# Sums of the first output chunks in the main stage, and the last batch's combine weights in the slot stage

## The chip, the cores and the metric

The kernel runs on one NeuronCore of a Trainium2 chip. TensorE (PE) multiplies, VectorE (DVE), ScalarE (ACT) and GpSimd (POOL) do the rest, and SyncE (SP) issues the transfers. The metric is the device time of one launch in microseconds, with all inputs in HBM at the start and the output there at the end. Everything is float32.

## The reference, cut to what matters

Agent attention over four batches of 11456 tokens (49 agents, 128 channels) is followed by a soft mixture of experts (32 slots, 8 experts) over all 45824 rows:

```python
def sm(a, b):
    s = scale * (a @ b.transpose(0, 2, 1))
    e = np.exp(s - s.max(-1, keepdims=True))
    return e / (e.sum(-1, keepdims=True) + 1e-09)
x = (sm(q, agents) @ (sm(agents, k) @ v)).reshape(B * S, D)
logits = x @ phi                                    # 45824 x 32
d = np.exp(logits - logits.max(0)); d /= d.sum(0) + 1e-09   # over the rows
slot_out[e] = np.maximum((d.T @ x)[e] @ w1[e], 0) @ w2[e]   # 8 experts, 4 slots each
c = np.exp(logits - logits.max(1)); c /= c.sum(1) + 1e-09   # over the slots
return c @ slot_out
```

The *combine weights* are c: for each row the maximum over 32 slots, the exponential, the sum and the division.

## The kernel before, in words

Rows are handled in *cells* of 128; a batch has 90 cells, so there are 360. The logits of all of them stay in SBUF as `x_all` (128 partitions, 360 cells, 32 slots), and become the combine weights in place.

The program has three stages.

- **Main stage.** For each of four batches, k and v come in groups of up to 20 cells (steps whose names begin with k) and q in 24 groups of up to 16 cells (names that begin with q, group number behind the @). `qs` multiplies q with the agents, `qt` transposes on DVE, `qm` takes the row maximum; in odd groups `qu` subtracts it on POOL, `qe` is the exponential on ACT and `qw` the sum on DVE; `qr` and `qR` are the reciprocal, `qg` the division on POOL, `qp`, `qc` and `ql` lead to the logits, `qM` and `qn` take their maximum and transpose them into `x_all`. `r1` to `r4` join the maxima of a round of one or two groups, `ru` subtracts on POOL, `re` is the exponential and `rg` multiplies into the slot sums. Of the k steps, `km` and `kM` are maxima, `kr` and `kR` the running maximum (`kR` writes `nm`), `ku` adds it, `kE` multiplies with v and `kA` accumulates.
- **Slot stage.** `nm`, `wt`, `gl`, `gm`, `l0` to `l4`, `f0` to `f2` and `d0` to `d2` join the slot sums of all batches; `l4` writes `si`, the slots' inputs. Then come the experts: `mh` (product with w1), `mr` (ReLU), `mt` and `mc` (transpose and copy), `mo` (product with w2), `sb` and `sd`; `sd` is an ACT instruction that writes `sob`, the scaled slot outputs, for which the first output product waits. `fl` are products that fill PE's waits.
- **Output.** 25 chunks of up to 16 cells (`CHUNKS` is 4, 12, then 21 times 16, 4, 4): four products with `sob` (tile `po`), copies out of PSUM on DVE (a quarter) and ACT (three quarters) into `ot`, and a transfer of up to 1 MB.

Around the combine weights there are these steps. `cr@i` takes the row maxima of group i (DVE, tile `rm`, or `rms` for the last batch, groups 18 to 23), `cu@i` subtracts them (POOL), and `ce@i` is the exponential (ACT). For the first seven output chunks (`NORM = 7`, 96 cells, all of the first batch and six cells of the second) `os@j` sums and inverts on DVE (`o_sum`: a TENSOR_REDUCE, a TENSOR_SCALAR that adds 1e-9, a RECIPROCAL; tile `cd`), `om@j` multiplies on POOL (`o_mul`), and for the first four `ot@j` transposes on DVE (`o_tr`, tile `ct`; the output buffer has the tile name `ot`). The later chunks do these three inside the output loop.

Every engine runs its own instructions in order. That order is written out by hand in the string `ORDER`, one token for each step; a step stands there after all that it depends on, and each engine gets its steps in that order. Buffers are given out along the same order.

Of the kernel before, what the change touches and what calls it, by code (L numbers as in the profile page):

```python
# [53 lines left out]
kM@3 kt kA qp.0@0 kr qx@3 qr@2 kt qR@2 qc.0@0 kR qg.0@2 kr qc.1@0 kb kR kn qg.1@2 ka@4 kb ku.0
qp.0@2 ka@3 kn ku.1 ke.0 kx@5 qp.1@2 qc.0@2 ku.0 kE.0@3 qc.1@2 ku.1 ke.1 qs.0@3 ke.1 ke.0
qs.1@3 kv@5 qt.0@3 kE.1 qt.1@3 qm@3 ks.0@5 kA qu@3 cx ks.1@5 km.0@5 qx@4 qe@3 kE.0@4 km.1@5
qw@3 kE.1 kM@5 qr@3 qR@3 kt kx@6 qg.0@3 kA kr kg.1 qg.1@3 kg.2 qp.0@3 kh.1 kh.2 kg.3 qs.0@4
kh.4 kh.3 kb kv@6 ql@0 qt.0@4 kn ql@1 ku.0 qc.0@3 qn.0@0 qs.1@4 ke.0 qM.0@1 qn.1@0 qM.0@0
kE.0@5 ku.1 qx@5 qM.1@0 ke.1 ks.0@6 qt.1@4 qm@4 kx@7 kE.1 km.0@6 qE.0 qM.1@1 ql@2 r1@0 kA r2@0
qn.0@1 ks.1@6 qM.1@2 qM.0@2 qn.1@2 kv@7 r3@0 qE.1 qp.1@3 qn.0@2 ru.0@0 km.1@6 qs.0@5 kM@6  # L60
qn.1@1 kt qt.0@5 ru.1 ks.0@7 kr kR cr@1 re.0@0 qr@4 qR@4 qx@6 re.1 cu@1 kb qs.1@5 km.0@7 kn
qc.1@3 rg.0@0 ku.0 qg.0@4 ka@6 rg.1 ce@1 ku.1 ql@3 ke.0 qg.1@4 qt.1@5 qp.0@4 ke.1 kx@8 qn.0@3
ks.1@7 qM.1@3 rc@0 qc.0@4 qm@5 qM.0@3 qu@5 r1@1 kE.0@6 km.1@7 qe@5 kM@7 cr@2 r2@1 kE.1 kv@8
r3@1 qn.1@3 ru.0@1 cr@3 qs.0@6 kA cr@0 cu@2 re.0@1 qs.1@6 qt.0@6 cu@0 qw@5 rg.0@1 ce@2 qx@7 kt
qt.1@6 ks.1@8 ru.1 ce@0 kr kR qr@5 qR@5 ka@7 qm@6 kb ks.0@8 cu@3 re.1 r4@1 kx@9 r4@0 kn qE.0
# [54 lines left out]
fl r4@11 qn.1@21 rg.0@10 qn.0@21 fl cr@21 ru.1 re.0@11 fl fl fl nm os@1 wt fl rg.0@11 cu@21  # L120
re.1 l0 fl f0 os@6 rc@11 f1 fl rg.1 om@1 ce@21 os@4 fl rc@10 fl gl om@6 ot@1 gm l1 d0 fl om@4
# [947 lines left out]
```

## Time and profile before

| | |
|---|---|
| Median of 3 runs | 320.97 us (319.19 to 323.69) |
| Profiled execution, its own time | 321.17 us |
| Its span, first to last instruction | 318.9 us |
| Mean granted TensorE clock | 0.931 |
| Busy share of the span | PE 84%, DVE 78%, ACT 59%, POOL 42% |
| Moved by the transfers | 104.20 MB, 23.59 MB of it the output |

Times in the rows below are microseconds from the span's start. A row of the timeline has start, duration, engine, line, operation, output<-input with shapes, count, and in brackets how long the engine had been idle before it and who released it. A row of the table by stretches has for each engine the busy time and the instructions in brackets, then PE's granted clock, the transfers' share of 16 DMA engines, and GB/s. Line numbers are those of the kernel before.

### The profile page before, as it was taken

The page shows a single profiled execution, that of the slowest core. Times are in us where ns is not written, and L with a number is a line of the kernel's source. Part 1 is how long each engine was busy: PE and PEld are TensorE (multiplying, and loading weights), DVE is VectorE, ACT ScalarE, POOL GpSimd, SP SyncE. Part 2 cuts the span into 40 slices and gives each one's busy share as a digit, 9 for nine tenths or more (in the row PEclk, how much of TensorE's full clock was granted, in tenths as well). Part 3 has the DMA queues.
Part 4 walks back from the last instruction along what each step waited for, and adds up shares of the span by engine and source line. Part 5 has one row for each costly group of instructions (what it writes and reads, how often), then busy time and mean ns, then how long its engine had stood idle before and what let it go on. Part 6 is the DMA issues. An engine that isn't in the chain of part 4 may idle for free.

```text
span 318.9 us, 11055 instructions
## 1 busy us (share of the span) xinstructions
PE 266.3 (84%) x4522; PEld 169.4 (53%) x4522; DVE 248.1 (78%) x598; ACT 189.4 (59%) x623; POOL 132.5 (42%) x166
## 2 busy tenths in 40 slices
PE   3799999997698998988999998998898876766850
PEld 3638668665554776664666775565574632111210
DVE  1357767897769986988999988988999659989830
ACT  1125791492754985558589568698663255655550
POOL 1012223064505552566444490476897404434300
PEclk9999999999989999999999999999999997767555
DMA  7999999999979999867996899746930049999997
GB/s 250 400 402 390 398 396 402 401 397 400 394 250 376 399 393 368 301 260 295 377 377 264 252 360 384 244 175 237 419 141 3 2 164 422 415 415 420 420 419 286
DMA packets 31298, 104.20 MB, mean 327 GB/s; under 512 B 3601, under 2 KB 7825, under 8 KB 27537
## 3 DMA queue, kind: packets, MB, share of 16 engines
q1 hardware_dynamic: 31248, 103.52, 84.4%
q8 instruction: 35, 0.57, 0.7%
q14 instruction: 15, 0.11, 0.1%
HBM read 79.91 MB, written 23.59 MB: 325 GB/s over the span
## 4 chain that ended last, share of the span: by engine, by line
PE 45%; DVE 26%; DMA 10%; ACT 9%; issue 5%; POOL 2%; SPq 0%; DVEq 0%; POOLq 0%; ACTq 0%
PE sk L252 10%; PE ev L351 8%; PE sq L466 8%; DMA out<-ot 7%; PE tp L522 5%; ACT pt L494 4%; PE po L1002 3%; DVE pt L472 3%; PE lq L535 3%; DVE kmx L305 2%; ACT ot L1007 2%; DVE cd L852 2%; DVE ot L1006 2%; DMA w1s<-w 2%; DVE mx L477 2%
## 5 line engine op out<-in xcount | busy, mean ns | idle before, releaser
L494 ACT ACTIVATE pt<-pt,mx 128x49 f32<-128x49 f32 x192 | 61.6, 329 | 10.2 <-DVE mx L477 10.2
L513 POOL TENSOR_TENSOR pt<-pt,rt 128x392 f32<-128x392 f32 (+1 forms) x48 | 38.7, 809 | 46.1 <-DVE rt L508 25.2
L252 PE MATMUL sk<-ag,kt 128*64 128x49 f32 x1440 | 51.7, 230 | 6.6 <-DMA kt<-kT 4.3
L252 PEld LDWEIGHTS sk<-ag,kt 128*64 128x64 f32 x1440 | 48.8, 145 | 11.6 <-DVE ag L183 4.1
L466 PE MATMUL sq<-qt,ag 128*32 128x512 f32 (+1 forms) x384 | 49.6, 607 | 1.8 <-DVE et L339 1.1
L1002 PE MATMUL po<-ct,sob 32*128 32x512 f32 (+2 forms) x200 | 37.8, 838 | 15.6 <-DVE ct L865 11.3
L351 PE MATMUL ev<-vt,et 128*64 128x129 f32 x720 | 46.8, 277 | 1.7 <-issue 1.4
L1007 ACT COPY ot<-po 128x1536 f32<-128x1536 f32 (+2 forms) x25 | 32.8, 1311 | 23.3 <-DVE ot L1006 23.2
L351 PEld LDWEIGHTS ev<-vt,et 128*64 128x64 f32 x720 | 40.3, 138 | 9.6 <-issue 5.6
L472 DVE STREAM_TRANSPOSE pt<-sq 128x512 f32<-128x512 f32 (+1 forms) x48 | 31.9, 669 | 12.5 <-PE sq L466 12.0
L635 POOL TENSOR_TENSOR dt<-x_all,mbs 128x512 f32<-128x512 f32 (+1 forms) x24 | 29.2, 1227 | 28.8 <-DVE mbs L626 24.9
L859 POOL TENSOR_TENSOR x_all<-x_all,cd 128x512 f32<-128x512 f32 (+2 forms) x25 | 24.0, 961 | 38.0 <-DVE cd L854 37.3
L482 POOL TENSOR_TENSOR pt<-pt,mx 128x784 f32<-128x784 f32 (+1 forms) x12 | 16.2, 1353 | 55.4 <-DVE mx L477 53.1
L494 ACT ACTIVATION_READ_ACCUMULATOR pt<-pt,mx 128x1 f32 x192 | 37.0, 193 | 0.0
L529 ACT COPY pT<-tp 128x512 f32<-128x512 f32 (+1 forms) x48 | 25.7, 557 | 13.1 <-PE tp L522 11.0
L1002 PEld LDWEIGHTS po<-ct,sob 32*128 32x128 f32 x200 | 10.8, 247 | 42.5 <-ACT ot L1007 42.1
L522 PE MATMUL tp<-cs,pt 128*128 128x128 f32 x180 | 27.9, 286 | 5.9 <-issue 4.2
L305 DVE TENSOR_REDUCE kmx<-sk 128x49 f32<-128x490 f32 x32 | 20.7, 658 | 13.8 <-PE sk L252 13.6
L344 ACT ACTIVATE et<-et 128x490 f32<-128x490 f32 x36 | 21.6, 619 | 11.2 <-DVE et L339 11.1
L522 PEld LDWEIGHTS tp<-cs,pt 128*128 128x128 f32 x180 | 19.5, 142 | 15.1 <-issue 9.0
L339 DVE TENSOR_TENSOR et<-sk,kmb 128x490 f32<-128x490 f32 x36 | 22.5, 653 | 2.9 <-ACT kmb L329 2.8
L1006 DVE COPY ot<-po 128x512 f32<-128x512 f32 (+2 forms) x25 | 15.7, 629 | 11.4 <-DMA out<-ot 7.5
(111 smaller groups left out, 396.6 us busy)
## 6 DMA issues: line engine op xcount, KB each, us to landing
out<-ot SPq DMA_DIRECT2D x21, 1024.0 KB, 7.4
qt<-qT SPq DMA_DIRECT2D x44, 448.0 KB, 7.4
vt<-vL SPq DMA_DIRECT2D x36, 451.5 KB, 7.4
kt<-kT SPq DMA_DIRECT2D x35, 448.0 KB, 6.7
kt<-kT SPq DMA_DIRECT2D x17, 384.0 KB, 6.9
vt<-vL SPq DMA_DIRECT2D x16, 387.0 KB, 8.1
w2s<-w SPq DMA_DIRECT2D x4, 1024.0 KB, 6.9
w1s<-w SPq DMA_DIRECT2D x4, 1024.0 KB, 10.5
```

The source lines that it names most:

```text
L252: t_.matmul(sp[r:r + 64, c - c0, :], xt[:, P * c + r:P * c + r + 64], ag[:, b, 0:A], start=True, stop=True)
L305: v_.tensor_reduce(out=o_, in_=sp.rearrange("p c a -> p a c"), axis=AX.X, op=ALU.max)
L351: t_.matmul(k["ev"][o_:o_ + 64, :], k["e"][:, c, :], k["v"][:, c, :], start=c < 2, stop=c >= n - 2)
L466: t_.matmul(q["s", h][32 * r_:32 * r_ + 32, :nt], ag[:, b, 32 * h:32 * h + 32], q["x"][:, r_, :], start=True, stop=True)
L472: v_.transpose(out=q["pt"][:, :n, 32 * h:32 * h + 32], in_=q["s", h][:, :nt].rearrange("p (t a) -> p t a", a=32))
L494: s_.activation(out=x, in_=x, func=AF.Exp, bias=q["mx"][:, c:c + 1], accum_out=q["dn"][:, c:c + 1])
L513: nc.gpsimd.tensor_tensor(out=x, in0=x, op=ALU.mult, in1=q["rt"][:, c0:c1].unsqueeze(2).to_broadcast([P, c1 - c0, A]))
L522: t_.transpose(q["tp", h][:, (c - c0) // 2, :], q["pt"][:, c:c + 2, :].rearrange("p c a -> p (c a)"), ident)
L529: s_.copy(out=q["pT"][:, c0 // 2:c1 // 2, :], in_=q["tp", h][:, :(c1 - c0) // 2, :])
L635: nc.gpsimd.tensor_tensor(out=q["dt"][:, :n], in0=q["lt"][:, :n, :], op=ALU.subtract, in1=mbs[:, ri, :].unsqueeze(1).to_broadcast([P, n, S]))
L1002: t_.matmul(po[:, r, :32 * n], z["sob"][32 * r:32 * r + 32, :], z["ct", j][32 * r:32 * r + 32, :32 * n], start=True, stop=True)
L1007: s_.copy(out=ov[:, 1:4], in_=po[:, 1:4, :32 * n])
```

## The change

Three things move; what is computed stays the same. (1) The seven `os` steps become two, each over 48 cells at once, into a kept tile `cds`, and both stand in the main stage, around q groups 10 to 12. (2) The seven `om` steps follow there one by one, between POOL's other steps up to group 15. (3) Of the last batch, `cr`, `cu` and `ce` of all six groups now come behind `l4`, among the experts' steps, and `ce@22` and `ce@18` directly ahead of `sd`. With them `ot@0` to `ot@3` stand just behind `l4`.

```diff
@@ ORDER, two pieces of it
-kb qp.1@7 km.1@12 kn qg.1@10 qp.0@10 kM@12
+kb qp.1@7 os@0 km.1@12 kn qg.1@10 qp.0@10 kM@12
...
-zz mo mc@51 mo ms mo sb ms sb fl fl sd
+zz mo mc@51 cr@22 cu@22 cr@18 cu@18 ce@20 ce@21 mo ms mo sb ms sb fl fl ce@22 ce@18 sd
@@ tiles
+    cds = keep.tile([P, C0[NORM]], F32, name="cds")
@@ steps
+    def o_sums(h):
+        n = C0[NORM] // 2
+        x = cds[:, n * h:n * h + n]
+        v_.tensor_reduce(out=x, in_=x_all[:, n * h:n * h + n], axis=AX.X, op=ALU.add)
+        v_.tensor_scalar(out=x, in0=x, scalar1=EPS, scalar2=None, op0=ALU.add)
+        v_.reciprocal(out=x, in_=x)
+        for j in range(NORM):
+            z["cd", j] = cds[:, C0[j]:C0[j] + CHUNKS[j]]
@@ dependences
-    for j in range(NORM):
-        ends_ = [k for k in ops if k[0] == "ce" and groups[k[1]][0] * NCELL <= C0[j] + CHUNKS[j]]
-        f = op("os", (j,), "V", 800, lambda j=j: o_sum(j), deps=ends_ + [ms])
-        f = op("om", (j,), "G", 1000, lambda j=j: o_mul(j), deps=(f,))
+    n = C0[NORM] // 2
+    ss = [op("os", (h,), "V", 2300, lambda h=h: o_sums(h), deps=done(n * h + n)) for h in range(2)]
+    for j in range(NORM):
+        f = op("om", (j,), "G", 1000, lambda j=j: o_mul(j), deps=ss[:1 + (C0[j] + CHUNKS[j] > n)])
```

Three places show what that does to the engines' rows.

DVE in the slot stage, from behind `nm` to `gl` before (three `os` with tile `cd`, `l0`, `f0` with tile `fd`, `gl`, `ot@1`):

```order
L852 TENSOR_REDUCE cd_4063<-x_all 128x12
L853 TENSOR_SCALAR cd_4063<-cd_4063 128x12
L854 RECIPROCAL cd_4063<-cd_4063 128x12
L772 TENSOR_SCALAR g_all<-gp_3984,wt 128x50
L757 TENSOR_SCALAR fd<-cs,wt 32x32
L852 TENSOR_REDUCE cd_4095<-x_all 128x16
L853 TENSOR_SCALAR cd_4095<-cd_4095 128x16
L854 RECIPROCAL cd_4095<-cd_4095 128x16
L852 TENSOR_REDUCE cd_4123<-x_all 128x16
L853 TENSOR_SCALAR cd_4123<-cd_4123 128x16
L854 RECIPROCAL cd_4123<-cd_4123 128x16
L734 TENSOR_TENSOR g_all<-g_all,wt 128x150
```

and the same place now, on to `l4` (the row of tile `si`):

```order
L715 TENSOR_REDUCE nmx<-m_all 128x1
L769 TENSOR_SCALAR g_all<-gp_3989,wt 128x50
L754 TENSOR_SCALAR fd<-cs,wt 32x32
L731 TENSOR_TENSOR g_all<-g_all,wt 128x150
L787 TENSOR_REDUCE gs_106<-g_all 128x1
L788 SCALAR_TENSOR_TENSOR gs_106<-gs_106,wt 128x1
L776 COPY gt<-gt_p 50x32
L762 TENSOR_TENSOR sie<-sie,fb 128x32
L783 TENSOR_TENSOR si<-si_p,sie 128x8x4
L872 STREAM_TRANSPOSE ct_3673<-x_all 128x128
```

Nothing of the combine weights is left between `nm` and `l4`. 

POOL in the main stage, the stretch around round 3 before (two `ru` with tile `dt`, two `cu`, then `qu@11` on `pt`):

```order
L635 TENSOR_TENSOR dt_2086<-x_all,mbs 128x512
L635 TENSOR_TENSOR dt_2105<-x_all,mbs 128x512
L563 TENSOR_TENSOR x_all<-x_all,rm_1919 128x512
L563 TENSOR_TENSOR x_all<-x_all,rm_2069 128x512
L482 TENSOR_TENSOR pt_2031<-pt_2031,mx_2097 128x10x49
```

and now:

```order
L632 TENSOR_TENSOR dt_2090<-x_all,mbs 128x512
L866 TENSOR_TENSOR x_all<-x_all,cds 128x128
L632 TENSOR_TENSOR dt_2110<-x_all,mbs 128x512
L560 TENSOR_TENSOR x_all<-x_all,rm_1920 128x512
L866 TENSOR_TENSOR x_all<-x_all,cds 128x384
L560 TENSOR_TENSOR x_all<-x_all,rm_2073 128x512
L479 TENSOR_TENSOR pt_2035<-pt_2035,mx_2102 128x10x49
```

`om@0` and `om@1` have come in between; the other five, `om@2` to `om@6`, stand each behind the second `qg` of groups 11 to 15.

ACT at the end of the slot stage before (`hs` is the ReLU `mr`, `ht` the copy `mc`, the rows of `x_all` are `ce`):

```order
L568 ACTIVATE x_all<-x_all 128x512
L813 ACTIVATE hs_4244<-hp_4215 128x512
L824 COPY ht_4257<-htp_4247 128x512
L847 ACTIVATE sob<-sb_p,dr 128x128
L1007 COPY ot_4344<-po_4339 128x384
```

and now:

```order
L821 COPY ht_4189<-htp_4174 128x512
L565 ACTIVATE x_all<-x_all 128x320
L565 ACTIVATE x_all<-x_all 128x512
L810 ACTIVATE hs_4216<-hp_4184 128x512
L821 COPY ht_4228<-htp_4218 128x512
L565 ACTIVATE x_all<-x_all 128x512 x4
L844 ACTIVATE sob<-sb_p,dr 128x128
```

Two exponentials stand ahead of the second ReLU of ACT, and four ahead of `sob`.

More of the change, by code (lines that the diff above doesn't have):

```diff
@@ L54 @@
[L54 to L65, printed above, removed]
@@ L120 @@
[L120 to L124 removed]
+kx@0 kx@1 ks.0@0 kv@1 km.0@0 kt kr kb ks.1@1 kn ku.0 qx@1 ke.0 ks.0@1 km.0@1 km.1@1 qx@0 kM@1 kt kr
@@ new lines @@
+qp.0@7 qe@9 kM@10 ru.0@2 qp.1@6 kA qr@8 re.1 qw@9 kg.2 qc.1@6 kg.1 qs.0@10 kh.1 cu@4 qR@8 re.0@2
+qr@9 qR@9 cr@5 qc.0@7 kg.3 qt.0@10 rg.0@2 qg.0@8 kx@11 ce@4 rg.1 kh.2 qs.1@10 rc@2 cu@5 kh.3 kh.4
+qg.0@9 kt ce@5 qt.1@10 qp.0@8 kr qg.1@9 qp.0@9 qm@10 qc.0@8 kb kv@11 qg.1@8 ql@6 kn qE.0 ku.0
+ks.0@12 qM.0@6 ku.1 ks.0@11 qn.0@6 km.0@12 qM.1@6 ke.1 qx@13 ks.1@11 km.0@11 ke.0 qn.1@6 qc.0@9
+kE.0@10 cr@6 qE.1 km.1@11 kE.1 qx@11 kM@11 kt kA ks.1@12 kr qx@12 qr@10 qR@10 kR qg.0@10 ka@11 kb
+qp.1@7 os@0 km.1@12 kn qg.1@10 qp.0@10 kM@12 qc.1@7 ku.0 kt kx@14 qs.0@11 ke.0 ku.1 kr ql@7 ke.1
@@ new lines @@
+qs.1@13 qE.1 qt.0@13 rg.0@4 qt.1@13 rg.1 kt qm@13 ks.0@14 kv@16 kr ce@8 qu@13 kR qr@12 qR@12 qc.0@11
+kb qs.0@14 km.0@14 kn rc@4 ka@13 qc.1@10 ku.0 qg.0@12 qp.1@11 qe@13 kt ku.1 ql@10 qg.1@12 om@3
+qc.1@11 qx@15 kr ke.1 qp.0@12 kR qn.0@10 ke.0 qM.0@10 ql@11 qM.1@10 qc.0@12 kb kE.0@13 qM.0@11 kn
+qM.1@11 ka@14 r1@5 qn.1@10 kx@15 cr@10 r2@5 kE.1 r3@5 qn.0@11 ru.0@5 ku.0 qs.1@14 kA ke.0 r4@5
+qn.1@11 cr@11 re.0@5 ru.1 qs.0@15 qt.0@14 qx@16 cu@11 rg.0@5 re.1 qw@13 qs.1@15 cu@10 ce@11 qr@13
+qR@13 rg.1 qt.1@14 kE.0@14 qg.0@13 rc@5 ce@10 qm@14 qx@20 qg.1@13 om@4 ks.1@15 kA qE.0 qt.0@15
@@ L125 @@
+mr@36 mh@39 mr@32 ot@2 cr@23 cu@23 mt@41 mt@37 mc@42 ot@3 cr@19 cu@19 mh@44 mc@38 mr@40 cr@20 cu@20
+cr@21 cu@21 ce@23 ce@19 mo mr@45 mt@46 mt@50 mc@47 zz mo mc@51 cr@22 cu@22 cr@18 cu@18 ce@20 ce@21
+mo ms mo sb ms sb fl fl ce@22 ce@18 sd
 """
@@ L953, in tile_agent_attn_soft_moe, with done @@
     o("sd", "A", 200, m_dr, deps=(b1, d2))
+    def done(c):
+        return [k for k in ops if k[0] == "ce" and
+                groups[k[1]][0] * NCELL + GROUPS[groups[k[1]][1]][0] < c]
+    n = C0[NORM] // 2
+    ss = [op("os", (h,), "V", 2300, lambda h=h: o_sums(h), deps=done(n * h + n)) for h in range(2)]
     for j in range(NORM):
-        ends_ = [k for k in ops if k[0] == "ce" and groups[k[1]][0] * NCELL <= C0[j] + CHUNKS[j]]
-        f = op("os", (j,), "V", 800, lambda j=j: o_sum(j), deps=ends_ + [ms])
-        f = op("om", (j,), "G", 1000, lambda j=j: o_mul(j), deps=(f,))
+        f = op("om", (j,), "G", 1000, lambda j=j: o_mul(j), deps=ss[:1 + (C0[j] + CHUNKS[j] > n)])
         if j < EARLY:
-            op("ot", (j,), "V", 650, lambda j=j: o_tr(j), deps=(f,))
+            op("ot", (j,), "V", 650, lambda j=j: o_tr(j), deps=(f, ms))
     f = None
```

122 lines of the change are left out of this document (58 added, 64 removed).

## The prediction

> **What bounds the kernel now.** I read the table by stretches first, from the place where the `os` and `cr` steps lie to the end.
>
> ```profile
> 224.80:235.10 10.30, 9.29 (x247) 6.29 (x247) 9.91 (x36) 5.86 (x15) 8.99 (x10) 1.00 0.89 367
> 235.10:244.40 9.30, 7.80 (x151) 6.11 (x147) 8.88 (x27) 3.60 (x8) 7.52 (x9) 1.00 0.01 4
> 244.40:249.00 4.60, 3.67 (x30) 1.39 (x30) 4.30 (x14) 1.64 (x3) 3.56 (x5) 1.00 0.01 4
> 249.00:256.80 7.80, 7.64 (x156) 5.90 (x157) 3.90 (x8) 2.58 (x5) 1.88 (x2) 1.00 0.01 2
> 270.00:280.00 10.00, 6.92 (x39) 2.11 (x40) 9.48 (x23) 5.76 (x4) 4.78 (x5) 0.77 1.01 419
> ```
>
> After 258 the output runs at the transfers' limit: their share is 1.01 at 419 GB/s, and 23.59 MB at that rate are 56 us. Nothing in the change touches that rate, and the moved steps issue no transfer, so SP's queue keeps its order. What counts is when the first output product starts, at 256.82 (its row stands below). From 225 to 249 DVE is over 93% busy in each stretch, and from 235 on the transfers are idle. PE waits for DVE four times:
>
> ```profile
> 226.70 1.06 PE L522 MATMUL tp<-cs,pt 128*128 128x128 f32 x8 [0.45 <-DVE x_all L552]
> 239.94 0.40 PE L762 MATMUL fb<-fd,cs 32*128 32x32 f32 x2 [0.56 <-DVE fd L757]
> 242.72 0.53 PE L730 MATMUL gt_p<-cs,g_all 128*50 128x32 f32 x8 [0.94 <-DVE g_all L734]
> 249.02 0.66 PE L818 MATMUL htp<-cs,hs 128*128 128x128 f32 x4 [0.95 <-DVE hs L811]
> ```
>
> The main stage is tighter. PE is busy 38 of 40 us and DVE 36:
>
> ```profile
> 160.00:200.00 40.00, 38.12 (x776) 25.96 (x772) 36.47 (x86) 31.31 (x132) 18.59 (x23) 1.00 0.90 324
> ```
>
> **Slot stage: what goes.** Ahead of `l4` DVE loses four `os`, six `cr` and one `ot`:
>
> ```profile
> 239.80 0.67 DVE L852 TENSOR_REDUCE cd<-x_all 128x16 f32<-128x512 f32 x1
> 240.50 0.17 DVE L853 TENSOR_SCALAR cd<-cd 128x16 f32<-128x16 f32 x1
> 240.71 0.25 DVE L854 RECIPROCAL cd<-cd 128x16 f32<-128x16 f32 x1
> 237.29 0.69 DVE L560 TENSOR_REDUCE rms<-x_all 128x16 f32<-128x512 f32 x1
> 248.31 0.66 DVE L811 TENSOR_SCALAR hs<-hp 128x512 f32<-128x512 f32 x1
> ```
>
> One `os` is 1.1 us and one `cr` 0.6, together about 8.5 us with the `ot`. The path gains less, because PE has its own work in order and is 90% busy up to 235. It gains its waits on DVE: 0.45 + 0.56 + 0.94 = 1.95 us until `l4`, which comes at 242.4 instead of 244.4. Behind `l4` DVE no longer has three `os` ahead of the ReLU at 248.31. `ot@0` and `ot@1` (0.7 together), now in that place, are done at 243.2, before PE has the ReLU's input at 244.5, so they cost nothing. The fourth wait, 0.95, goes: PE's `mt@37` comes at 246.0 instead of 249.02, 2.9 us earlier. POOL loses seven `om` and six `cu` there, so `ru`, `re` and `rg` ahead of `gl` are not late either.
>
> **What is late next.** Now `cr`, `cu` and `ce` of the last batch lie there. These rows price them (`cu` on POOL, `ce` and `sob` on ACT, and PE's `mh` and three `mo` beside them):
>
> ```profile
> 238.80 1.05 POOL L563 TENSOR_TENSOR x_all<-x_all,rms 128x512 f32<-128x512 f32 x1
> 249.61 1.07 PE L805 MATMUL hp<-w1s,si 128*32 128x512 f32 x8
> 252.50 2.83 PE L834 MATMUL so_p<-w2s,ht 128*32 128x128 f32 x96
> 250.20 0.63 ACT L568 ACTIVATE x_all<-x_all 128x512 f32<-128x512 f32 x1
> 256.27 0.37 ACT L847 ACTIVATE sob<-sb_p,dr 128x128 f32<-128x128 f32 x1 [3.51 <-PE sb_p L844]
> 256.82 1.15 PE L1002 MATMUL po<-ct,sob 32*128 32x128 f32 x16
> ```
>
> DVE finishes `ot@3` at about 247.4 and `cr@19` at 248.0; `cu@19` ends at 249.0 and `ce@19` at 249.6. ACT's second ReLU is queued behind it and ends at 250.15, while PE, with 0.6 for `mt`, 0.9 for `mh`, 0.95 for each `mo` (of the second it does thirteen of sixteen pieces first), reaches `mt@50`, which needs it, at 249.75: a new wait of 0.4. `mt@50` then ends at 250.75, DVE's `mc@51` at 251.4, `cr@22` at 252.0; `cu@22` and `cu@18` end at 253.05 and 254.05, `ce@18` at 254.7. `sob` is queued behind `ce@18` on ACT. PE would allow it at 253.7 (experts end at 252.9, then copy and `sb`); it comes at 255.0 and the first output product at 255.2. So of 2.9 us **1.6 remain**, from 256.82 to 255.2. The ends: all 2.9 if the new chain is quicker, nothing if each step of it slips by 0.4.
>
> **Main stage: what is added.** A reduction of 1536 elements is in no row. The nearest are
>
> ```profile
> 146.77 0.97 DVE L477 TENSOR_REDUCE mx<-pt 128x16 f32<-128x784 f32 x1
> 247.20 0.97 DVE L853 TENSOR_SCALAR cd<-cd 128x4 f32<-128x4 f32 x1
> ```
>
> From 512 to 784 elements it grows by 0.30 us, so 1536 give about 1.8 (three times 0.67 is 2.0 at most, 0.97 the least). With 0.2 for the addition and 0.4 for 48 reciprocals one `os` is 2.4 us. Two waits of DVE lie where they are put, and a third follows:
>
> ```profile
> 124.83 0.67 DVE L305 TENSOR_REDUCE kmx<-sk 128x49 f32<-128x490 f32 x1 [1.77 <-PE sk L252]
> 140.59 0.35 DVE L357 SCALAR_TENSOR_TENSOR acc<-acc,al,ev 128x129 f32<-128x129 f32 x1 [1.22 <-PE ev L351]
> 144.08 0.67 DVE L305 TENSOR_REDUCE kmx<-sk 128x49 f32<-128x490 f32 x1 [0.59 <-PE sk L252]
> ```
>
> `os@0` hides 1.77 of itself and leaves 0.6. Ahead of `os@1` POOL comes in. There `om@0` and `om@1` (0.4 and 0.8, by the rows below) stand in a stretch of POOL without a gap, and `qu@11`, its last, is waited for by ACT's `qe@11` and DVE's `qw@11`:
>
> ```profile
> 239.81 0.83 POOL L859 TENSOR_TENSOR x_all<-x_all,cd 128x384 f32<-128x384 f32 x1
> 248.47 0.40 POOL L859 TENSOR_TENSOR x_all<-x_all,cd 128x128 f32<-128x128 f32 x1 [0.32 <-DVE cd L854]
> 130.75 2.51 POOL L635 TENSOR_TENSOR dt<-x_all,mbs 128x512 f32<-128x512 f32 x2 [5.86 <-DVE mbs L626]
> 133.33 2.06 POOL L563 TENSOR_TENSOR x_all<-x_all,rm 128x512 f32<-128x512 f32 x2
> 135.35 1.02 POOL L482 TENSOR_TENSOR pt<-pt,mx 128x490 f32<-128x490 f32 x1
> 136.40 0.62 ACT L487 ACTIVATE pt<-pt 128x490 f32<-128x490 f32 x1 [0.23 <-POOL pt L482]
> 137.06 0.67 DVE L499 TENSOR_REDUCE dn<-pt 128x10 f32<-128x490 f32 x1
> ```
>
> So `qw@11` slips by 1.2, and with it all that is queued behind it on DVE. The sum to 144: 0.6 + 1.2 + 2.4, less the waits of 1.22 and 0.59, is 2.4 us. From there DVE runs without a gap, and PE waits for it:
>
> ```profile
> 149.50 0.32 PE L259 MATMUL mc<-cs,nm 128*64 128x49 f32 x4 [1.39 <-DVE dn L504]
> 147.97 1.38 DVE L321 TENSOR_TENSOR nm<-nr,nm 128x1 f32<-128x1 f32 x1
> 147.82 1.52 POOL L482 TENSOR_TENSOR pt<-pt,mx 128x784 f32<-128x784 f32 x1 [2.50 <-DVE mx L477]
> 150.79 0.85 POOL L513 TENSOR_TENSOR pt<-pt,rt 128x392 f32<-128x392 f32 x1
> 151.98 0.16 DVE L321 TENSOR_TENSOR nm<-nr,nm 128x1 f32<-128x1 f32 x1
> ```
>
> The same `nm` takes 0.16 us with POOL idle and 1.38 while POOL works on SBUF: it ends when `qu` ends, at 149.35. `om@3` now follows the `qg` that ends at 151.64 and runs to 152.7; `nm` of 151.98 falls into it and waits some 0.6. [...]
>
> `om@2`, `om@4` and `om@6` fall into waits of POOL, and so do most of their neighbours; I cost them at nothing, and at up to 0.5 each if a `qg` comes behind them. Two of PE's own waits have no releaser in the profile; the later one, and the end of the last k product, are
>
> ```profile
> 196.36 1.60 PE L252 MATMUL sk<-ag,kt 128*64 128x49 f32 x47 [0.93 <-issue]
> 215.86 1.32 PE L351 MATMUL ev<-vt,et 128*64 128x129 f32 x20
> ```
>
> If that wait does not move with the rest it swallows up to 0.93 of the delay; I take half. Main stage: 2.4 + 0.6 - 0.5 = **2.5 us later**. The ends: 0.6, if only the rest of `os@0` counts, and 6.6 with both `os` (4.8), the POOL delay (1.2) and the port wait (0.6) wholly on the path.
>
> **The sum** is +2.5 - 1.6 = +0.9 us. Against the profiled execution's own time, 321.17 (its span of 318.9 and 2.3 around it), that is 322.1; the median of the runs is 0.2 lower, so I forecast **322.0 us**. A change of less than 2% (6.4 us) is about what a measurement of this kernel cannot tell from none; the three runs alone spread over 4.5 us.
>
> **Rivals.**
>
> 1. *The main stage swallows the delay.* PE is 95% busy there with work of its own, and DVE's waits at 140 and 144 show that it runs ahead at places. Then only 0.6 is left and the slot stage gives 1.6 to 2.9: 318.9 to 320.2, about 319.5. Against it: DVE has no gap from 144 to 161.
> 2. *The wait changes its name* (slower). `sob` waits for `ce@18`, the end of a chain over three engines, just as late as PE waits for DVE now. It decides when `ce@18` ends behind 256.3, which takes 1.6 us more than my walk: one further `cu` of 1.05 ahead of it and one copy of 0.6 will do. Then the main stage's 2.5 us stand alone: 323.7.
> 3. *It does not do what it says*: DVE's total barely falls (two `os` for seven save 7.5 - 4.8 = 2.7 us), and if both stages are bound by PE's own order the time is that of before, 321.
>
> **How the numbers follow.** Forecast (321.5 to 323) 0.40, rival 1 0.32, rival 2 0.15, rival 3 0.10. The remaining 0.03 are cases over 2%: slower needs all of 6.6 us and no gain (327.8); faster would need 6.4 us, and all four of PE's waits give only 2.9. The range takes in both rivals and the ends near them, 318.0 to 325.0. Faster by over 2%: 0.01, within 2%: 0.97, slower: 0.02.
>
> **What would show it.** In the profile after: the waits on `fd`, `g_all` and `hs` gone and `l4` 2 us earlier relative to the end of the k groups; ACT's `sob` directly behind a `ce`, with POOL busy on `cu` until 254; `os` rows of 2.4 us with no wait of DVE behind them; POOL's `qu@11` 1.2 later, PE's wait behind it longer, an `nm` near 0.8 us beside an `om`; the main stage's last k product, which ended at 217.2 (the row of 215.86), ending near 219.7. Wrong would make it a main stage that ends where it did, or a first output product that starts before 254 or after 259.

## The result, and the profile after

| | before | after |
|---|---|---|
| Median of 20 runs each | 320.85 us (318.63 to 323.99) | 323.83 us (320.63 to 328.00) |
| Ratio | | 1.0074, 95% interval 1.0047 to 1.0100 |
| Profiled execution, own time | 321.17 us | 322.73 us |
| Its span | 318.9 us | 320.8 us |

The change makes the kernel 2.4 us slower (0.74% of 320.9; the interval is 1.5 to 3.2 us). That is less than 2%, as forecast, on the forecast's side of zero, and inside the range. The forecast was +0.9 us. Ratios and their intervals here and below go by fast executions alone, those less than 1.5% above the fastest of their kernel (16 of the 20 of the changed kernel, four each in e6 and e9), and e10's profiled execution was a slow one.

To compare stages between executions I use marks that every version has: the tenth and the last `acc` of the k groups on DVE, and the first output product. Up to the tenth `acc` all versions run the same program, and yet it comes between 107.1 and 109.9 us in thirteen executions. A stage's price is therefore read from mark to mark and not from the span's start. The first two rows are of before, the next two of after, from the timeline:

```profile
109.15 0.35 DVE L357 SCALAR_TENSOR_TENSOR acc<-acc,al,ev 128x129 f32<-128x129 f32 x1
217.29 0.35 DVE L357 SCALAR_TENSOR_TENSOR acc<-acc,al,ev 128x129 f32<-128x129 f32 x1 [0.84 <-PE ev L351]
```

```profile
107.90 0.34 DVE L354 SCALAR_TENSOR_TENSOR acc<-acc,al,ev 128x129 f32<-128x129 f32 x1
219.97 0.35 DVE L354 SCALAR_TENSOR_TENSOR acc<-acc,al,ev 128x129 f32<-128x129 f32 x1 [0.84 <-PE ev L348]
```

From mark to mark the **main stage** took 108.14 us before and 112.07 after: 3.9 us more. By the span's start it looks like 2.7, because the same program had come to the first mark 1.25 us earlier this time. Where the time goes stands around the two `os`, in the timeline of after:

```profile
121.72 1.74 DVE L850 TENSOR_REDUCE cds<-x_all 128x48 f32<-128x1536 f32 x1
123.50 0.19 DVE L851 TENSOR_SCALAR cds<-cds 128x48 f32<-128x48 f32 x1
123.72 0.45 DVE L852 RECIPROCAL cds<-cds 128x48 f32<-128x48 f32 x1
...
135.71 1.02 POOL L479 TENSOR_TENSOR pt<-pt,mx 128x490 f32<-128x490 f32 x1
137.42 0.66 DVE L496 TENSOR_REDUCE dn<-pt 128x10 f32<-128x490 f32 x1 [1.22 <-ACT pt L484]
139.66 1.71 DVE L850 TENSOR_REDUCE cds<-x_all 128x48 f32<-128x1536 f32 x1
141.41 0.75 DVE L851 TENSOR_SCALAR cds<-cds 128x48 f32<-128x48 f32 x1
142.19 0.45 DVE L852 RECIPROCAL cds<-cds 128x48 f32<-128x48 f32 x1
142.56 0.25 DVE L354 SCALAR_TENSOR_TENSOR acc<-acc,al,ev 128x129 f32<-128x129 f32 x1
142.96 1.09 PE L519 MATMUL tp<-cs,pt 128*128 128x128 f32 x4 [2.84 <-DVE acc L354]
154.31 0.68 DVE L318 TENSOR_TENSOR nm<-nr,nm 128x1 f32<-128x1 f32 x1
```

`os@0` takes 2.4 us and the `kmx` behind it no longer waits. `qu@11` (the row of 135.71) stands 27.8 us behind the first mark; it was 26.2 before. DVE now waits 1.22 us for `qw@11`. The addition of `os@1` takes 0.75 us instead of 0.19, beside POOL's `om@2`. Behind `os@1` stands `kA` (the `acc`), which frees the buffer for the transposes of group 11, and PE waits 2.84 us for it. What follows is in the table by stretches, in the column before the transfers' share:

```profile
140.00:142.00 2.00, 0.12 (x2) 0.00 (x0) 1.97 (x2) 0.62 (x1) 2.00 (x4) 1.00 0.14 44
142.00:144.00 2.00, 1.04 (x6) 0.74 (x6) 1.97 (x5) 0.28 (x2) 0.11 (x1) 0.71 0.00 0
144.00:146.00 2.00, 2.00 (x39) 2.00 (x40) 1.31 (x3) 2.00 (x15) 1.23 (x1) 0.50 0.00 0
146.00:148.00 2.00, 2.00 (x24) 0.74 (x24) 1.44 (x3) 2.00 (x12) 1.09 (x2) 0.94 0.35 74
```

PE is busy 0.12 of the first two microseconds, and right behind that the granted clock falls to 0.50. The missing clock is 2 x (0.29 + 0.50 + 0.06) = 1.7 us, that is 3.4 us at half speed. None of this stood in the prediction.

The **slot stage** (last `acc` to first output product) fell from 39.53 to 38.61 us, 0.9 less. In the timeline of after, PE's and DVE's rows, then ACT's and POOL's, then the first output product:

```profile
243.69 0.53 PE L727 MATMUL gt_p<-cs,g_all 128*50 128x32 f32 x8 [0.17 <-DVE g_all L731]
245.40 0.19 DVE L783 TENSOR_TENSOR si<-si_p,sie 128x32 f32<-128x32 f32 x1 [0.86 <-PE si_p L780]
253.43 0.65 PE L815 MATMUL htp<-cs,hs 128*128 128x128 f32 x4 [0.38 <-ACT hs L810]
255.55 2.05 POOL L560 TENSOR_TENSOR x_all<-x_all,rms 128x512 f32<-128x512 f32 x2 [1.07 <-DVE rms L557]
256.63 0.63 ACT L565 ACTIVATE x_all<-x_all 128x512 f32<-128x512 f32 x1 [1.48 <-POOL x_all L560]
257.64 0.63 ACT L565 ACTIVATE x_all<-x_all 128x512 f32<-128x512 f32 x1 [0.37 <-POOL x_all L560]
258.17 0.35 ACT L844 ACTIVATE sob<-sb_p,dr 128x128 f32<-128x128 f32 x1
258.58 1.15 PE L1013 MATMUL po<-ct,sob 32*128 32x128 f32 x16 [1.07 <-ACT sob L844]
```

The wait on `g_all` fell from 0.94 to 0.17, those on `fd` and `hs` (DVE) are gone, the new wait of 0.38 at `mt@50` is there, and `sob`, which had waited 3.51 us for PE, now starts directly behind `ce@18`. PE waits 1.07 us for it. The output stage took 62.2 us (62.1 before).

### The profile page after: what moved, and what is told of

Same layout as the page of the kernel before. It is cut to its first block, busy times and chain, and to the rows that moved or that the text cites. A ratio compares the mean times of both kernels' runs of the same rounds, so it can differ in the third digit from the quotient of the medians.

```text
span 320.8 us, 11038 instructions
## 1 busy us (share of the span) xinstructions
PE 265.9 (83%) x4522; PEld 172.5 (54%) x4522; DVE 246.4 (77%) x583; ACT 189.3 (59%) x623; POOL 132.3 (41%) x166
## 4 chain that ended last, share of the span: by engine, by line
PE 39%; DVE 28%; DMA 11%; ACT 11%; POOL 5%; issue 4%; SPq 0%; DVEq 0%; POOLq 0%; ACTq 0%
PE sk L249 8%; DMA out<-ot 7%; PE ev L348 7%; PE sq L463 7%; ACT pt L491 5%; PE tp L519 4%; PE lq L532 2%; DVE pt L469 2%; PE po L1013 2%; DMA qt<-qT 2%; DVE ot L1017 2%; DVE mx L474 2%; DVE cm L544 2%; POOL x_all L560 2%; PE gp L645 2%
## 5 line engine op out<-in xcount | busy, mean ns | idle before, releaser
L249 PE MATMUL sk<-ag,kt 128*64 128x49 f32 x1440 | 52.8, 233 | 7.3 <-DMA kt<-kT 4.5
L249 PEld LDWEIGHTS sk<-ag,kt 128*64 128x64 f32 x1440 | 50.0, 148 | 12.5 <-DVE ag L179 4.1
L463 PE MATMUL sq<-qt,ag 128*32 128x512 f32 (+1 forms) x384 | 50.6, 592 | 2.2 <-DVE et L336 1.1
L1013 PE MATMUL po<-ct,sob 32*128 32x512 f32 (+2 forms) x200 | 35.1, 783 | 19.4 <-DVE ct L872 12.8
L491 ACT ACTIVATION_READ_ACCUMULATOR pt<-pt,mx 128x1 f32 x192 | 36.3, 189 | 0.0
L526 ACT COPY pT<-tp 128x512 f32<-128x512 f32 (+1 forms) x48 | 25.6, 555 | 12.3 <-PE tp L519 10.2
L866 POOL TENSOR_TENSOR x_all<-x_all,cd 128x512 f32<-128x512 f32 (+1 forms) x18 | 17.6, 976 | 30.7 <-DVE cd L861 30.7
```

The source lines that it names most:

```text
L249: t_.matmul(sp[r:r + 64, c - c0, :], xt[:, P * c + r:P * c + r + 64], ag[:, b, 0:A], start=True, stop=True)
L463: t_.matmul(q["s", h][32 * r_:32 * r_ + 32, :nt], ag[:, b, 32 * h:32 * h + 32], q["x"][:, r_, :], start=True, stop=True)
L491: s_.activation(out=x, in_=x, func=AF.Exp, bias=q["mx"][:, c:c + 1], accum_out=q["dn"][:, c:c + 1])
L526: s_.copy(out=q["pT"][:, c0 // 2:c1 // 2, :], in_=q["tp", h][:, :(c1 - c0) // 2, :])
L1013: t_.matmul(po[:, r, :32 * n], z["sob"][32 * r:32 * r + 32, :], z["ct", j][32 * r:32 * r + 32, :32 * n], start=True, stop=True)
```

## The experiments

All times of stages are from one profiled execution each. The last column says where the granted clock stood at 0.50 between the two marks of the main stage.

| kernel | main | slot | output | ratio to before, 95% | half clock |
|---|---|---|---|---|---|
| before | 108.14 | 39.53 | 62.1 | 1 | none |
| after | 112.07 | 38.61 | 62.2 | 1.0074 (1.0047 to 1.0100) | 142-147 |
| e1_main_only | 111.06 | 36.50 | 62.6 | 1.0044 (1.0002 to 1.0085) | none |
| e2_slot_only | 108.13 | 40.10 | 62.1 | 1.0030 (0.9994 to 1.0067) | none |
| e3_sob_first | 112.36 | 37.68 | 62.1 | 1.0034 (0.9996 to 1.0073) | 144-149 |
| e4_om_in_gap | 112.40 | 38.78 | 62.0 | 1.0050 (1.0013 to 1.0088) | 200-204 |
| e5_cr_late_os_slot | 107.29 | 36.84 | 63.7 | 0.9961 (0.9929 to 0.9993) | none |
| e6_cr_late | 114.60 | 36.63 | 64.9 | 1.0121 (1.0075 to 1.0167) | 142-150 |
| e7_no_om | 109.03 | 38.66 | 62.2 | 1.0010 (0.9977 to 1.0043) | none |
| e8_act_copies | 107.89 | 36.85 | 64.2 | 0.9919 (0.9882 to 0.9957) | none |
| e9_fill5 | 110.64 | 39.59 | 62.7 | 1.0100 (1.0030 to 1.0171) | none |
| e10_os_behind | 111.52 | 38.61 | 62.2 | 1.0057 (1.0026 to 1.0088) | 200-204 |
| e11_again | 111.82 | 38.67 | 62.1 | one run | 143-148 |

Four executions of the old main stage (before, e2, e5, e8) lie between 107.3 and 108.1 us, mean 107.86.

**One part alone.** `e1_main_only` and `e2_slot_only`:

```diff
 e1: os, om as in the changed kernel; cr, cu, ce @18-23 and ot in their old places
-zz mo mc@51 cr@22 cu@22 cr@18 cu@18 ce@20 ce@21 mo ms mo sb ms sb fl fl ce@22 ce@18 sd
+zz mo mc@51 mo ms mo sb ms sb fl fl sd
 e2: cr, cu, ce @18-23 as in the changed kernel; seven os, om and ot in their old places
-kb qp.1@7 os@0 km.1@12
+kb qp.1@7 km.1@12
```

> The sums and multiplications of the first seven chunks stand in the main stage as in the changed kernel; cr, cu, ce of the last batch and the ot stay where they stood before. My theory: the main stage ends 2.5 to 2.7 us later than before, and the slot stage, rid of seven os and with no exponential queued ahead of sob, gains the PE's waits on DVE, 1.9 to 2.9 us; in all 0 to +0.8 against the kernel before, about 321.3 us. Rival (PE's own order bounds the slot stage): nothing comes back, +2.7, about 323.6. Rival (the main stage swallows the delay): -1.5 to -2.5, about 319.

> cr, cu, ce of the last batch stand behind l4 as in the changed kernel; the seven os, om and the ot stay in the slot stage as before. My theory: the main stage ends as before (217.2 for the last k product). Ahead of l4 only the cr are gone, four os stay, so about 1 us of PE's 1.95 us of waits remains; behind l4 DVE has three os (3.4 us) and six cr (3.6 us) beside the experts, where it had 2.3 us idle in the changed kernel, so the chain cr, cu, ce ahead of sob ends about 1 us later than in that kernel relative to l4. In all between -0.5 and +1.0 against before, about 321. Rival (the slot stage gains by the moved cr alone what it gained in the changed kernel): -0.9, about 320.

The first output product, e1 above, e2 below:

```profile
255.40 1.15 PE L1013 MATMUL po<-ct,sob 32*128 32x128 f32 x16
```

```profile
255.99 1.15 PE L998 MATMUL po<-ct,sob 32*128 32x128 f32 x16 [1.05 <-ACT sob L843]
```

Taking the `os` out of the slot stage gives 3.0 us there (39.53 to 36.50), and costs 3.2 us in the main stage (111.06 against 107.86). Moving `cr`, `cu`, `ce` behind `l4` gives nothing: 0.6 more than before (40.10), with the wait for `sob` of 1.05; on top of e1 it costs 2.1 (36.50 to 38.61). So neither part pays, and the second takes back most of what the first gains in the slot stage. Ahead of `l4` both parts go for the same waits: `l4` comes 27.15 us behind the last `acc` before, 25.92 in e2, 25.31 in e1 and 25.43 with both. Behind `l4` e2 takes 14.18 us to the first output product, before 12.38. Both measured ratios are above 1, e2's by less than it is uncertain.

**`sob` ahead of the last two exponentials.**

```diff
-mo ms mo sb ms sb fl fl ce@22 ce@18 sd
+mo ms mo sb ms sb fl fl sd ce@22 ce@18
```

> The changed kernel with ce@22 and ce@18 behind sd on ACT instead of ahead of it; nothing else. My theory (sob is late because two exponentials are queued ahead of it): sob starts 1.07 us earlier, PE's wait of 1.07 us ahead of the first output product goes; the two exponentials (1.26 us) now stand ahead of ACT's first output copy, which had waited 1.02 us, so 0.2 is given back: -0.8 us against the changed kernel, about 323.0. Rival (the output is bound by its transfers from their first one on, and that comes no earlier): no change.

```profile
258.71 0.37 ACT L844 ACTIVATE sob<-sb_p,dr 128x128 f32<-128x128 f32 x1 [1.96 <-PE sb_p L841]
258.98 1.14 ACT L565 ACTIVATE x_all<-x_all 128x512 f32<-128x512 f32 x2
259.26 1.15 PE L1013 MATMUL po<-ct,sob 32*128 32x128 f32 x16
260.22 0.48 ACT L1018 COPY ot<-po 128x384 f32<-128x384 f32 x1
```

ACT now waits for PE ahead of `sob`, and PE no longer for `sob`: the slot stage is 0.9 us shorter (37.68, against 38.61 to 38.78 in after, e4, e7, e10 and e11). The exponentials stand behind it, with no idle time of ACT ahead of its first copy. The order on ACT was worth what the trace said; the times (1.0034 against 1.0074, overlapping intervals) point the same way and do not settle it.

**POOL's part in the main stage.**

```diff
 e4
-kM@12 ... qg.1@10 qp.0@10       (om@0 to om@3 among round 3 and behind groups 11, 12)
+kM@12 ... qg.1@10 om@0 om@1 om@2 om@3 qp.0@10
 e7, o_mul
+        if j < NORM:
+            return
```

> The changed kernel with om@0 to om@3 in the gap that POOL has between qg of group 10 and the ru of round 3 (5.86 us in the kernel before, 3.33 us needed); nothing else. My theory (of the 2.7 us of the main stage, POOL's om make 1.2 by delaying qu@11, 0.56 by holding the addition of os@1, and 0.52 by holding nm): the main stage ends 1.2 to 2.2 us earlier than in the changed kernel, about 322. Rival (the DVE time of the two os, 4.8 us against 3.6 us of waits, is the price, and DVE has no gap behind them whatever POOL does): 0 to -0.5, about 323.5. [...]

> The changed kernel without the seven om: rows of the first seven chunks are not divided by their sums. The os stay. My theory by now (the DVE time of the two os is the price of the main stage, not POOL's om): from the tenth to the last acc 110 us or more, where the kernel before has 108.13 and the one with the main-stage part alone 111.06: at most 1 us of 2.9 goes. My prediction's theory (POOL's om make 1.2 of it by delaying qu@11, and 1.1 by stalls of DVE beside om): 108.8 us, 2.3 of 2.9 go. A stretch at half the granted TensorE clock in that part would add about 1.5 us to either.

Without `om` the main stage takes 109.03 us, 2.0 less than e1 with the same two `os`. My doubt had been wrong and the prediction's own step right: POOL's seven products, not DVE's sums, are the larger part of the price, and the sums alone cost 109.03 - 107.86 = 1.2 us (one execution each, and the four of the old main stage differ by 0.85 among themselves). The 2.0 lie between the twelfth and the fourteenth `acc` (28.15 us in e1, 26.02 in e7), where `qu@11`, the addition of `os@1` and `nm` are. In e4 that stretch takes 26.01 us too; so the gap does take the four `om` out of the way there. It gives the gain back at two places, so that the 1.2 to 2.2 us that I expected did not come (PE's matmul at 159 is from e4; the `mxs` first from e4, then from e1, where no `om` is beside it):

```profile
126.61 3.20 POOL L866 TENSOR_TENSOR x_all<-x_all,cds 128x128 f32<-128x128 f32 x4 [0.62 <-DVE cds L852]
127.09 0.78 DVE L305 TENSOR_TENSOR mxs<-kmx 128x49 f32<-128x49 f32 x1
159.17 2.02 PE L463 MATMUL sq<-qt,ag 128*32 128x512 f32 x5 [0.32 <-DMA qt<-qT]
```

```profile
124.68 0.21 DVE L305 TENSOR_TENSOR mxs<-kmx 128x49 f32<-128x49 f32 x1
```

`mxs` takes 0.57 us longer beside them (0.78 against 0.21), as `nm` did elsewhere (0.68 in after, 0.16 before), and from the tenth to the twelfth `acc` e4 takes 1.1 us longer than e1 (22.53 against 21.42); between the fourteenth and fifteenth `acc` 0.8 us go (6.13 against 5.32), where PE has caught up with a load of q. The half clock at 200 to 204 adds 1.6 us more in this execution (18.38 us from the seventeenth to the eighteenth `acc`, 16.75 in e1).

**The half clock.** Five fillers ahead of the transposes that waited, `os@1` two steps later, and the changed kernel once more:

```diff
 e9
-qp.1@10 km.0@13 qE.0 qg.1@11 om@2 qp.0@11
+qp.1@10 km.0@13 qE.0 qg.1@11 om@2 fx fx fx fx fx qp.0@11     (fx: z_fl, as fl)
 e10
-ks.0@13 os@1 kA qm@12 qg.0@11
+ks.0@13 kA qm@12 os@1 qg.0@11
```

> The changed kernel with five filler products (2.2 us of PE at full clock) ahead of the first transposes of group 11, where PE had waited 2.84 us for DVE, which was busy with os@1; in the executions of this main stage with the wait of 2.3 to 2.8 us the granted TensorE clock fell to 0.50 for 3.4 us right behind it, and the stretch to the next acc took 16.4 us instead of 14.9. My theory (the idle time of PE brings the clock down): no stretch at 0.50 between 140 and 152, twelfth to fourteenth acc as in the execution without it (28.1 us), from the tenth to the last acc 111 us, and 0.5 to 1.5 us less than the changed kernel in the mean of the runs, about 323. Rival (the clock falls for another reason, or the time went to the wait itself): the stretch at 0.50 is there as before, 112 us, 324. Either way the two fillers too many cost at most 0.5.

> The changed kernel with os@1 two steps later on DVE, behind kA (which frees the buffer for which PE waited 2.84 us) and qm of group 12, instead of ahead of them. My theory (the main stage pays for the place of os@1, since PE stands still behind it and its clock falls): PE's wait of 1.2 to 2.8 us there goes, no stretch at 0.50 between 140 and 152, and the part from the tenth to the last acc falls to 109.5 to 110.5 us, so 1 to 2 us less than the changed kernel, about 322. Rival (DVE's own total is the price, since it has no gap from 144 to 161): PE only waits a little later, 111 us, 323 to 324.

> The changed kernel once more, one look. Three of the four executions of its main stage showed the granted clock at 0.50 between 142 and 149 us. My theory (it follows a wait of PE of over 2 us, so depends on how the loads come in ahead of it): it is there if PE's wait for acc is over 2 us, and the stretch from the thirteenth to the fourteenth acc is then about 16.4 us; if the wait is nearer to 1.2 us, it is not there, and the stretch is 14.9 us. Rival: the two have nothing to do with each other.

The table by stretches of e9, and then the waiting transposes in e1, e3 and e11, one row each:

```profile
140.00:142.00 2.00, 1.87 (x17) 1.63 (x16) 1.93 (x5) 0.00 (x0) 1.07 (x2) 1.00 0.03 11
142.00:144.00 2.00, 2.00 (x48) 1.71 (x52) 1.97 (x4) 1.32 (x9) 0.28 (x1) 1.00 0.00 0
144.00:146.00 2.00, 1.78 (x23) 0.35 (x19) 1.94 (x5) 2.00 (x12) 1.92 (x2) 1.00 0.56 141
```

```profile
142.90 0.63 PE L519 MATMUL tp<-cs,pt 128*128 128x128 f32 x4 [1.19 <-DVE acc L354]
```

```profile
144.03 0.63 PE L519 MATMUL tp<-cs,pt 128*128 128x128 f32 x4 [2.29 <-DVE acc L354]
```

```profile
143.30 0.63 PE L519 MATMUL tp<-cs,pt 128*128 128x128 f32 x4 [2.02 <-DVE acc L354]
```

With a wait of 2.84 (after), 2.29 (e3), 2.29 (e6) or 2.02 us (e11) the clock fell to 0.50 within 0.8 us of its end; with 1.19 (e1), 1.40 (e4) or 1.12 (e7) and without the wait (e10) it did not. The stretch from the thirteenth to the fourteenth `acc` takes 16.4 us with one drop (16.38, 16.48, 16.44), 17.9 in e6, where it lasted twice as long, and 14.91 in e1 and in e9, while the stretch ahead of it takes 13.23 to 13.26 us in all six. So a drop costs 1.5 us there. How long the wait is, is decided ahead of it: at 138 PE stands for something that the profile doesn't name, not at all in after, 0.61 us in e3 and e6, 0.89 in e11 and 1.71 in e1, and together with the wait for `acc` that is 2.8 to 2.9 us each time.

Whether filling the wait takes the drop away, e9 does not show, since its execution is of the kind of e1:

```profile
137.19 1.65 PE L348 MATMUL ev<-vt,et 128*64 128x129 f32 x25 [1.55 <-issue]
140.03 0.66 PE L519 MATMUL tp<-cs,pt 128*128 128x128 f32 x4
140.53 1.26 PE L878 MATMUL fl<-cs 128*128 128x128 f32 x10
141.91 0.63 PE L519 MATMUL tp<-cs,pt 128*128 128x128 f32 x4
```

PE had already stood 1.55 us ahead of 137.19, and from the end of the first transposes (140.69) to the second, which start when the `acc` is there, it is 1.2 us. So the fillers stand in the short wait, and behind that e1 had no drop without them. e10 took the wait away and had no drop there, in one execution. That the drop hangs on the wait therefore rests on the comparison of these executions, and on the steps shown in the last section.

In the timed runs e9 is no faster than the changed kernel (1.0100 against 1.0074, with a wide interval), where 0.5 to 1.5 us less was expected. Its slot stage took 39.59 us, 1.0 more than the changed kernel's; all of it lies ahead of `l4` (26.40 us behind the last `acc`, 25.43 in after), where PE waits 0.76 us for ACT's `dt`, and why that is late I have not traced (buffers are given out along the order, so five fillers shift them). e10's drop at 200 is another one, as in e4, behind a wait of 1.77 us that has no releaser in the profile; with it the main stage took 111.52 us, not the 109.5 to 110.5 expected, and about 110 without its 1.5. Its 1.0057 lies inside the interval of the changed kernel.

**Out of the slot stage altogether.** `e6` takes the six `cr`, `cu`, `ce` into the output loop, one group at every second chunk from the fifth; `e5` does this with the old main stage and the `os` in the slot stage; `e8` is e5 with ACT copying those six chunks whole.

```diff
 e5, e6, output loop
+            if 16 + j // 2 in lates and j % 2 == 0:
+                for f in lates[16 + j // 2]:        # cr, cu, ce of one group
+                    f()
 e5, ORDER
-d1 os@2 mh@35 d2 cu@20 ce@18 os@5 mh@31 mr@36 os@0 om@5
+ot@1 os@2 om@2 ot@0 d1 mh@35 d2 mh@31 mr@36 mh@39 mr@32 os@4 om@4
 e8, output loop, for those chunks
-            v_.tensor_copy(out=ov[:, 0], in_=po[:, 0, :32 * n])
-            s_.copy(out=ov[:, 1:4], in_=po[:, 1:4, :32 * n])
+            s_.copy(out=ov, in_=po[:, :, :32 * n])
```

> Nothing of the sums stands in the main stage: the seven single os and om are in the slot stage, three of them ahead of l4, two among the experts, two behind the last copy; cr, cu, ce of the last batch are taken out of the slot stage and done inside the output loop, one group at every second chunk from the fifth on. My theory: the main stage has the length of before (108.13 us from the tenth to the last acc of DVE, in two executions of that program), and with seven os but no cr the slot stage falls from 39.5 us (last acc to first output product) to 36.5 to 37.5, as in the kernel with the main-stage part alone, which had six cr but no os; the output stays at 62.1 us, since DVE is some 6 us ahead of the last transfer: -2.0 to -3.0 against before, about 318. Rival (DVE, busy 95% in the first half of the output, falls behind the transfers by the 3.7 us of cr): 0 to +1.

> The changed kernel, with cr, cu, ce of the last batch inside the output loop as in the other kernel of this call; os and om stay in the main stage. My theory (the three instructions behind l4 cost the slot stage 2.1 us: 1.1 of sob behind ce@18, 0.4 of the ReLU behind ce@19, the rest DVE's copies and ReLU behind cr): last acc to first output product falls from 38.6 to 36.5 us, -2.1 against the changed kernel, so +0.5 against before, about 321. Rival (only sob behind ce@18 costs anything): -1.0, 37.6 us.

> The kernel with the os in the slot stage and cr, cu, ce inside the output loop, and in addition ACT copies the whole of the six output chunks at which a cr is done, instead of three quarters of them, which takes DVE's copy of 0.65 us away there. My theory (the output stage lost 1.6 us because DVE, with 2.3 us of work for each chunk and 0.6 to 1.0 more for each cr, was slower than the transfers' 2.5 us): DVE then needs 4.9 us for two chunks and the transfers 5.0, so the output lasts 62.1 to 62.6 us again and the whole is 2.2 to 2.7 us faster than before, a ratio of 0.992. Rival (something else delays the output there, ACT or POOL): 63.7 us as in that kernel, a ratio of 0.996.

The slot stage falls to 36.6 to 36.9 us in all three, as expected: `cr`, `cu` and `ce` behind `l4` cost 2.0 us, and seven `os` with no `cr` beside them cost 0.3 (36.84 against 36.50). But the output became longer, 63.7, 64.9 and 64.2 us. In e5's loop and table:

```profile
258.04 0.66 DVE L555 TENSOR_REDUCE rms<-x_all 128x16 f32<-128x512 f32 x1
259.33 0.59 DVE L852 TENSOR_SCALAR cd<-cd 128x16 f32<-128x16 f32 x1
...
284.00:288.00 4.00, 3.39 (x16) 0.54 (x8) 3.74 (x10) 2.93 (x3) 2.00 (x3) 0.58 0.88 363
```

Each `cr` takes DVE 0.66 to 0.68 us (the last group's 0.46, in e8), and the addition that follows it, with the `cu` started on POOL, takes 0.4 us longer (0.59 to 0.60, where the next one takes 0.17); the transfers' share falls to 0.88 (before, in the same stretch, 1.02). That this work of DVE is what lengthens the output is argued, not shown: e8 takes a copy of 0.65 us off DVE at each of these chunks, and its output is no shorter. Of e5's 2.7 us in the slot stage the output leaves 1.1. e6 loses more in the output (2.7) than it gains in the slot stage, and its main stage held the drop of double length: it is 1.2% slower than before, where +0.5 us was expected. e8, the best version here, is 0.8% faster than before (2.6 us, 1.4 to 3.8) and beats both kernels; its interval overlaps e5's. That it is faster because the output is short again is not shown: its profiled output took 64.2 us, as the rival has it.

## Why the prediction was right, and where its sizes were off

**Direction and sum.** +0.9 was forecast, 2.4 measured (1.5 to 3.2). Both terms had the right sign; main stage 2.5 and slot stage -1.6 turned out 4.2 (112.07 against the mean of 107.86) and -0.9. Their sum is 3.3 in an execution with the drop of the clock and 1.8 without its 1.5; the 2.4 of the runs lies between, as it would if the drop falls into some executions only.

**Main stage: the sum of rows was nearly right.** One `os` is 2.4 us, as estimated from two rows. `qu@11` comes 1.6 us later from the mark, of which 1.2 are the two `om` (in e7, without them, it stands 26.65 us behind the mark, 27.81 in after); `nm` took 0.68 (forecast near 0.8). e7 shows POOL's share as 2.0 us; the prediction had 1.2 + 0.6, which is as near as that partly by luck, since a part was missing. Missed: the addition of `os@1` stands beside `om@2` and takes 0.56 longer (0.75 against 0.19), although the prediction's own row of 247.20 shows such an addition: 0.97 us for 4 sums, where one for 16 takes 0.17. Beside it POOL has a product:

```profile
247.10 1.05 POOL L859 TENSOR_TENSOR x_all<-x_all,cd 128x512 f32<-128x512 f32 x1 [0.72 <-DVE cd L854]
```

The reduction of 1536 elements ahead of it took 1.71 us with POOL busy throughout. No run shows a port, by whose name the prediction counts 0.6 us for `nm`; what the runs show is that `nm` took 0.68 us beside `om@3` in after, and 0.16 with POOL idle before. The wait at 196 that was to swallow 0.5 swallowed nothing: it is 0.92 us in after, 0.93 before, and from the fourteenth `acc` to the last it is 61.2 us in the mean of the four executions of the old main stage and 61.4 in the six of the new one (with `om`) that have no drop there. Without a drop of the clock the term is 2.8 to 3.2 us (e9, e1) against 2.5.

**The step that failed there** is the one that followed DVE alone behind `os@1`. `kA` stands behind `os@1`; the prediction named the wait of `qw@11` but not who waits for `kA`. PE does, 2.84 us, and the half clock behind that cost 1.5 us, a term that the prediction has at nothing. That is the larger part of the error in this term. Taking DVE's own waits off was right: the `kmx` of 144.08 before, 34.93 us behind the first mark, comes 37.36 behind it in e1, without the drop. That is 2.4 us later, the prediction's sum to this place. In after it waits for PE and comes 3.6 later (e1, then after):

```profile
145.20 0.66 DVE L302 TENSOR_REDUCE kmx<-sk 128x49 f32<-128x490 f32 x1
```

```profile
146.40 0.67 DVE L302 TENSOR_REDUCE kmx<-sk 128x49 f32<-128x490 f32 x1 [1.06 <-PE sk L249]
```

The prediction spoke of two waits of PE without a releaser; between the marks three are longer than 0.9 us (at 124.00, 138.79 and 196.36). The one at 138.79, 1.44 us, is not in its sum, and it is the one that trades with the wait for `kA`.

**Slot stage: the mechanism was right, its end a little too early.** `l4` came 25.43 us behind the last `acc`, 27.15 before: 1.7 earlier, forecast 2.0. e1, with the `cr` in their old places, has it at 25.31, so the six `cr` in the prediction's 8.5 us gave nothing ahead of `l4` once the `os` were gone. The new wait at `mt@50` is 0.38 (0.4). `sob` directly behind `ce@18` costs 0.9 to 1.1 us (e3's stage; the wait), forecast 1.3. The mis-sized term behind `l4` is what the `cr` cost PE ahead of that: 0.4 was counted, for `mt@50`. From `si` to the first product e3 takes 1.1 us longer than e6, which has no `cr` there (12.3 against 11.2). The walk followed ACT's queue, and gave DVE's ReLU and copies behind `ot@3` and `cr` no delay of their own.

**Rivals.** The main stage swallowed nothing, so rival 1 is out, and e1 shows it directly. Rival 2 was half of the truth: the wait changed its name from DVE to `sob`, but only for 1.07 us. Rival 3 is out: both stages moved.

**Shown and not shown.** Shown by a kernel each: POOL's share (e7), the price of the place of `sob` (e3), that both parts are losses or at best even (e1, e2), and that `cr` behind `l4` costs 2 us (e6). Shown by comparing executions, without a kernel that settles it: that the drop comes with PE's long wait. Not settled: what PE stands for at 138, which decides how long the wait for `acc` is, and how often the drop comes (in four of the five executions of this main stage with all its steps in their places).

## What to carry to other kernels

Before a long step is put into an engine's idle time, list what is queued directly behind it and which buffer that frees: a wait of DVE that hides a sum may be the time in which DVE was ready for PE. A clock that falls behind such a wait of PE adds to the price (1.5 us here). Work that nobody needs yet (here the weights of the last batch) belongs behind the instruction that the next stage waits for, not ahead of it in the same queue, and not into a stage whose engine has only 0.2 us a chunk to spare. And compare two executions between marks of the program: by the span's start the main stage's price was hidden by 1.25 us of scatter in code that had not changed.

## What the runs showed of the hardware that was not expected

A wait of PE of 2.0 to 2.8 us, far from the output stage, was followed by 3.4 us or more at a granted clock of 0.50, four times out of four at this place, and not behind waits of 1.12 to 1.40. The drop lasted 3.4 us in after, e3 and e11 and 6.8 in e6.

The place of the wait goes with it too, and the traces show a grid. In each of the ten executions in which two drops or more can be placed (before, after, e1, e3, e4, e6, e7, e9, e10, e11) all of these start on one grid of 3.41 us, the length of a single drop: in after at 16.54, 74.57 and 142.83, which lie 17.0 and 20.0 such steps apart. These are the steps at the wait for `acc`, in after (a drop follows) and in e1 (none):

```profile
139.41:142.82 3.41, 0.71 (x7) 0.42 (x4) 3.34 (x6) 0.63 (x1) 2.70 (x5) 1.00 0.21 76
```

```profile
139.45:142.86 3.41, 2.26 (x52) 1.97 (x48) 3.34 (x6) 0.63 (x1) 2.60 (x5) 1.00 0.27 98
```

Between 4 and 250 us PE was busy 21 to 53% of the step ahead of each of the 24 drops, and 46% or more of every other step at full clock in the executions that have a drop there (for the experiments an estimate from their tables in stretches of 1 us). e2 has none up to 250 us; by the same estimate, wherever steps of 3.41 us are laid in it, PE is busy at most 45% of one. So in these executions a drop went with about half a step of idle time or more, and that much was not always followed by one.

The length of a wait alone did not decide it. Ahead of the first mark the program is the same in before and after, and PE's waits at 14 to 17 us are nearly alike: 1.75 and 0.67 us in before, up to 15.49 and 16.85, and 1.76 and 0.67 in after, up to 15.28 and 16.38. After has a drop at 16.54, and PE was busy 29% of the step ahead of it (from 13.13). The grid of before, counted back from its drop at 86.91, cuts at 11.82, 15.23 and 18.64; PE is busy 56 and 73% of the two steps, and there is no drop. And in e2 a wait of 2.30 us at 84 had no drop behind it (granted clock 1.00 from 4 to 250 us), where one of 2.32 in before had (86.91 to 90.33, the step ahead 32% busy).

The same addition on DVE took 0.19 us with POOL idle (144.23 in e10, POOL busy 0.00 us from 144 to 145) and 0.75 beside a product on POOL (141.41 in after). The reductions over 512 elements (`cr`) took 0.63 to 0.69 us in after with POOL busy or idle, and the reciprocals of ten elements 0.21 to 0.22.
